# A hand-written planner learns to model three DMA queues, and takes its order of work from tables

## The chip, the cores and the metric

The kernel runs on one core of a Trainium2 chip. A core has five engines that run side by side, each through its own list of instructions in order: TensorE (PE: matmuls; its weight loads are shown as PEld), VectorE (DVE), ScalarE (ACT), GpSimd (POOL, which here only builds two index tiles and issues loads) and SyncE (SP, which here only issues stores and transposes by DMA). They wait for each other through semaphores. The metric is the device time of one execution in microseconds, lower is better.

## The reference

Causal attention with a sliding window and a few global keys, followed by a two-layer feed-forward net. Four batches, eight heads, 768 tokens, 64 numbers a head; 3072 tokens of width 512 go into the net, whose hidden width is 2048.

```python
scores = scale * np.matmul(q, k.transpose(0, 1, 3, 2))
keep = is_global | is_local              # 8 global keys, 96 keys back
scores = np.where(keep, scores + bias, -1000000000.0)
a = np.exp(scores - np.max(scores, axis=-1, keepdims=True))
a = a / (np.sum(a, axis=-1, keepdims=True) + 1e-09)
x = np.matmul(a, v)                      # to 3072 x 512
h = np.maximum(x @ w_in, 0.0)
out = h * h @ w_out
```

## The kernel before, in words

The 768 tokens of a batch are cut into six tiles of 128; three tiles make a half (eight halves, numbered 0 to 7, `hb` in the code). For a half, q and k are loaded (POOL, lines 395 on) and turned so that a head's 64 numbers lie on the partitions: halves 0, 1 and 2 on PE (`turn_tile`, `turn`), later ones by DMA transposes on SP's queue (`turn_by_dma`). `score_unit` multiplies q and k, ACT takes the exponential, DVE multiplies by a mask, `attend` multiplies with v, DVE divides by the sum (`norm`), and SP transposes the result by DMA into `xt` (`to_x_by_dma`, line 684). `layer1` multiplies by `w_in`, ACT or DVE take the positive part and the square; `layer2` multiplies by `w_out`, and SP stores. A part of layer 1 and most of layer 2 go through seven half-size products in place of eight (`layer1_group`, line 809, `layer2_pair`, line 1044), with sums of weights and of activations made by DVE.

The first two halves are done tile by tile (`OPENING`): `score_tile` first puts the distance bias into PSUM with matmuls of a diagonal (`slope_id`, line 1250) and then adds the scores (line 1257); `attend_tile`, `tile_to_x` (turned on PE) and pieces of layer 1 follow. `w_in` comes in four quarters (line 456).

Nobody writes the order of the instructions down: `Plan.run` does. It is a list scheduler that runs while the kernel is built. Every piece of work is an `Op` with a cost for each engine that could do it, what it needs, which ring of buffers and which of the eight PSUM banks it takes, and a rank. At each step the planner takes, among all ops whose needs are planned, the one that can start first by its own clock, with the rank as the tie-break, picks the engine that ends it first, and emits its instructions. PE's jobs and the loads are kept in two queues in the order in which they were listed (`merge`, `PLACES`, `LAYER1`, `OPENING`, `LOADING`), and only a queue's head can be planned. A DMA is modelled by a fixed lag, a fixed duration after the last one, and 2.8 us more when loads are under way (`crowd`). Before 24 us of the planner's clock, gaps in front of PE jobs are filled with dummy matmuls (`warm`, lines 281 and 284).

PE changes between matmuls that contract over 128 rows and the scores, which contract over 64 rows in pairs. Buffers named below: `ex`, `ph0` and `phat` hold weights of the attention, `hr` and `h2` the hidden layer, `y` the output, `w_mix` and `in_mix` sums of weights.

Of the kernel before, what the change touches and what calls it, by code (L numbers as in the profile page):

```python
# [13 lines left out]
P = 128  # L14
# [39 lines left out]

class Op:
    EARLY = {"ACT": 0.035, "DVE": 0.045}
    LATE = {"ACT": 0.1, "DVE": 0.07}

    def __init__(self, costs, emit, needs, rank=0, lag=0.0, land=None, slots=()):
        self.emit, self.rank, self.lag, self.land = emit, rank, lag, land  # L60
        self.needs = [n for n in needs if n is not None]
        self.costs = {e: c - self.EARLY.get(e, 0.0) for e, c in costs.items()}
        self.slots = slots
        self.done, self.bufs = None, []
        self.crowd = 0.0
        self.wait = 0.0
        self.shy = {}
# [12 lines left out]

class Plan:
# [8 lines left out]
    HOP = 0.08  # L90

    def __init__(self, warm_from, warm_until):
        self.warm_from, self.warm_until = warm_from, warm_until
        self.queues = {"PE": [], "LOAD": []}
        self.rest = []
        self.free = {e: 0.75 for e in ("ACT", "DVE", "POOL", "SP")}
        self.landed = 4.2
        self.rank = 0
        self.banks = [[] for _ in range(8)]
        self.rings = {}  # L100

    def pe(self, cost, emit, needs=(), takes=0, lag=0.24):
        self.rank += 1
        op = Op({"PE": cost}, emit, needs, self.rank, lag)
        op.takes, op.users = takes, [[op] for _ in range(takes)]
# [10 lines left out]
    def add(self, costs, emit, needs=(), rank=None, wait=0.0):  # L116
        rank = self.rank if rank is None else rank
        op = Op(costs, emit, needs, rank + RANKS.get(emit.__name__, 0))
        op.wait = wait
# [3 lines left out]
    def load(self, dur, emit, needs=(), rank=None, lag=2.6, hop=1.45):  # L123
        rank = self.rank + 0.5 if rank is None else rank
        op = Op({"POOL": 0.92}, emit, needs, rank, lag, land=dur)
        op.hop = hop
# [20 lines left out]
    def ready(self, op):  # L147
# [3 lines left out]
        for n in op.needs:  # L151
            if n.done is None:
                return None
            t = max(t, n.done + self.HOP)
        if getattr(op, "takes", 0):
# [11 lines left out]

    def run(self):
        order = []
        while self.rest or any(self.queues.values()):  # L170
# [13 lines left out]
            taken = self.idle_banks(op.takes) if getattr(op, "takes", 0) else []  # L184
            self.free[e] = end
            op.done = end + op.lag + op.LATE.get(e, 0.0)
            if op.crowd and self.landed > end + 0.3:
                op.done += op.crowd
                self.landed += getattr(op, "dma", 0.0)
            if op.land is not None:  # L190
                self.landed = max(end + op.hop, self.landed) + op.land
                op.done = self.landed + op.lag
# [20 lines left out]
def kernel(  # L213
# [169 lines left out]
    def list_loads(x, first=None):  # L383
# [5 lines left out]
        vbefore = [halves[x.hb - x.half - 3].attended[-1]] if x.hb >= 4 else []  # L389

        def rows(src, name, t, rank=None):
# [10 lines left out]
            if x.hb > 2:  # L402
                return plan.load(1.12, emit, vbefore if name == "v" else before, rank, 1.3, 0.7)
            return plan.load(0.86, emit, vbefore if name == "v" else before, rank,
                             1.6 if x.hb == 0 else 2.6)

        if x.half == 0:
# [3 lines left out]
            x.bt.op = plan.add({"DVE": 0.1}, start, vbefore, rank=0)  # L411
# [22 lines left out]
    def first_tiles(x, dst, src, eng, e, lags):  # L434
        casts = []
        for i, lag in enumerate(lags):
# [7 lines left out]
            op = plan.add({e: 0.5}, start, rank=-1)  # L444
            op.lag = lag
# [8 lines left out]
    def load_w_in(c):  # L454
        n = d_ff // 4
        w_in_op[c] = plan.load(2.55, lambda e: nc.gpsimd.dma_start(
# [3 lines left out]
    def list_w_out(first):  # L460
        n = NFT // 4
        for c in range(4):
            w_out_op.append(plan.load(2.55, lambda e, c=c: nc.gpsimd.dma_start(
# [33 lines left out]
    def fix_v(bt, t0, t1):  # L497
# [9 lines left out]
        if BY_DMA[2 * batches.index(bt) + t0 // HT]:  # L507
            op = plan.add({"SP": 1.2}, values_by_dma, needs, wait=4.0)
            op.lag, op.crowd, op.dma = 2.2, 2.8, 0.5
        else:  # L510
            op = plan.add({"DVE": 0.62} if bt is batches[0] else {"DVE": 0.62}, values,
                          needs, wait=0.0 if bt is batches[0] else 4.0)
# [36 lines left out]
    def turn_by_dma(x):  # L549
        late = list(halves[x.hb - 2].x_ops.values()) if x.hb > 3 else []  # L550
        for i, (name, loads) in enumerate((("sk", x.k_in), ("sq", x.q_in))):
# [7 lines left out]
            op = plan.add({"SP": 1.6}, emit, [*x.k_in, *x.q_in, x.bt.op, *late])  # L559
            op.lag = 3.4  # L560
# [3 lines left out]
        def fix(e):  # L564
# [5 lines left out]
                      x.turned[:1], wait=4.0)  # L570
# [12 lines left out]
    def score(x, k):  # L583
        for unit in [UNITS[x.half][u] for u in TOGETHER[x.half][k]]:
            score_unit(x, unit, unit[0] == UNITS[x.half][TOGETHER[x.half][k][0]][0])

    def score_unit(x, unit, fresh):
# [12 lines left out]
        job = plan.pe(0.182 * fresh + 0.057 * 4, emit,  # L600
                      [o for a in {a for a, _, _ in unit} for o in x.qk_ops[a]], 2)
# [76 lines left out]
    def to_x_by_dma(x, a):  # L678
# [8 lines left out]
        x.x_ops[a] = plan.add({"SP": 1.3}, emit, [norm])  # L687
        Buffer("tm", 6).used_by(norm, x.x_ops[a])
        x.xt_buf.used_by(x.x_ops[a])
        x.x_ops[a].lag, x.x_ops[a].crowd = 1.8, 2.8  # L690


    def layer1(x, ms, c0=0, c1=HALF, k0=0, k1=NCT):
# [3 lines left out]
        def emit(e):  # L697
            if x.h2 is None:
                x.h2 = h_p.tile([P, NFT, HALF], FP16, name="h2", tag="h2")
# [3 lines left out]
            for i, m in enumerate(ms):  # L703
                for kk in range(k0, k1):
# [6 lines left out]
                       for o in [x.x_ops.get((a, t), x.x_ops.get(a))]] + [w_in_op[ms[0] // 4]],  # L711
                      int(k0 == 0))
# [24 lines left out]
        if len(ms) > 1 or ms[0] % 2:  # L737
            m0 = ms[0] // 2 * 2 if len(ms) == 1 else ms[0]

            def square(e):  # L740
                hr = pair["hr"][:, 0:width * n].rearrange("p (m c) -> p m c", c=n)
                h2 = x.h2[:, m0:m0 + width, c0:c1]
# [52 lines left out]
    def layer1_group(x, g):  # L795
# [5 lines left out]
        def product(name, fresh, left, right, needs):  # L801
            def emit(e):
                if x.h2 is None:
                    x.h2 = h_p.tile([P, NFT, HALF], FP16, name="h2", tag="h2")
# [58 lines left out]
        def give(job, name, which, n, kept=None):  # L863
# [42 lines left out]
            def square(e):  # L906
                hr, h2 = hidden(which), x.h2[:, m0 + which * far:m0 + which * far + 2]
# [50 lines left out]
    def layer2(x, j, m0):  # L958
        st = x.l2.setdefault(j, {})

        def emit(e):
            if m0 == 0:
                st["ps"] = bank([P, 512], FP32, "yps")
            for m in range(m0, m0 + 4):
# [3 lines left out]
                      + [w_out_op[m0 // 4]], int(m0 == 0))  # L968
# [6 lines left out]
        if m0 + 4 == NFT:  # L975
# [5 lines left out]
            store = plan.add({"SP": 0.6}, lambda e: nc.sync.dma_start(  # L981
# [531 lines left out]
```

## Time and profile before

| what | us |
|---|---|
| median of 3 runs (203.25 to 204.84) | 203.93 |
| profiled execution, first to last instruction (span) | 202.3 |
| PE busy / DVE / ACT / POOL | 194.4 / 172.8 / 146.1 / 66.8 |
| first matmul starts (a dummy) | 1.67 |
| last matmuls (16 of line 1161) start | 198.08 |

The profiled execution is known by its span alone; the median of the runs lies 1.6 us above it. A PE matmul's own duration (273 ns for 128x256) is longer than its place in the stream, since matmuls are pipelined: eight of them that start at 196.33 are followed by the next eight at 197.21, so one takes 0.110 us of PE. Read the same way from rows that follow each other, a matmul takes 0.162 us of PE at 384 columns, 0.109 at 256, 0.082 at 192, 0.056 at 128, 0.216 at 512, 0.030 for the 65 columns of the attention, and 0.028 for one of the scores' pairs. The granted clock of PE was 1.00 over the traced span, but its first dummies follow each other at 0.106 us and, from 5.4 us on, at 0.056.

Busy shares by stretch, from the windows of the trace:

| us | PE | DVE | ACT | GB/s |
|---|---|---|---|---|
| 0 to 20 | 16.44 of 20 | 14.88 | 16.41 | 169 |
| 20 to 40 | 19.67 | 18.45 | 17.32 | 182 |
| 80 to 100 | 19.21 | 18.03 | 16.56 | 153 |
| 100 to 120 | 19.93 | 19.86 | 17.18 | 157 |
| 140 to 160 | 20.00 | 19.28 | 16.52 | 56 |
| 180 to 203 | 19.14 of 23 | 13.83 | 9.41 | 58 |

### The profile page before, as it was taken

How to read it: one execution, taken by the hardware profiler on the slowest of the kernel's cores; microseconds unless marked ns; L12 is line 12 of the kernel's file. 1: busy time of each engine (PE TensorE's matmuls, PEld its weight loads, DVE VectorE, ACT ScalarE, POOL GpSimd, SP SyncE). 2: the span in 40 equal slices, each digit the busy share in tenths (PEclk: the TensorE clock that was granted, in tenths of full speed). 3: DMA queues.
4: the chain of work that ended last, by engine and by line, in shares of the span. 5: the costliest groups of instructions: out<-in, count | busy, mean ns of one | idle time of the engine just before them, and what ended most of it. 6: DMA issues, size and time to landing. Idle time of an engine off the chain costs nothing.

```text
span 202.3 us, 5784 instructions
## 1 busy us (share of the span) xinstructions
PE 194.4 (96%) x2292; PEld 159.2 (79%) x2292; DVE 172.8 (85%) x455; ACT 146.1 (72%) x308; POOL 66.8 (33%) x82
## 2 busy tenths in 40 slices
PE   6798999999999999998999999999999999999993
PEld 6577887965897777777788878997788788987883
DVE  7569979999996798987999999998899979288922
ACT  6799998699522999968888797748886952478220
POOL 7996638077009600940680059000000000000000
PEclk9999999999999999999999999999999999999999
DMA  5999999999999998999999999993232023110123
GB/s 161 176 150 191 198 178 155 199 206 163 176 162 143 204 182 168 108 181 170 156 134 157 162 169 134 161 173 84 41 105 75 3 66 99 52 55 0 52 107 104
DMA packets 106491, 27.12 MB, mean 134 GB/s; under 512 B 96992, under 2 KB 103520, under 8 KB 106464
## 3 DMA queue, kind: packets, MB, share of 16 engines
q0 software_dynamic: 74944, 13.11, 91.2%
q1 hardware_dynamic: 30320, 13.05, 32.0%
q10 hardware_dynamic: 1200, 0.59, 1.1%
q8 instruction: 18, 0.29, 0.6%
q14 instruction: 9, 0.07, 0.1%
HBM read 27.26 MB, written 6.29 MB: 166 GB/s over the span
## 4 chain that ended last, share of the span: by engine, by line
PE 74%; DMA 12%; DVE 6%; POOL 4%; issue 1%; ACT 0%; POOLq 0%; DVEq 0%
PE yps L1044 31%; PE hps L705 21%; PE hps L809 11%; DMA w_in_sb<-in_moe_w_in_dram 6%; PE sp L598 4%; DMA w_mix<-in_q_dram 4%; PE av L659 3%; PE yps L965 3%; DMA xt<-tm 2%; POOL v L395 1%; POOL w_mix L395 1%; DVE hr L867 1%; DVE h L746 1%; PE trp L535 1%; DVE tm L669 1%
## 5 line engine op out<-in xcount | busy, mean ns | idle before, releaser
L705 PE MATMUL hps<-xt,w_in_sb 128*128 128x384 f16 (+2 forms) x432 | 62.8, 290 | 1.0 <-DVE tm L669 0.7
L705 PEld LDWEIGHTS <-w_in_sb 128*128 128x128 f16 x432 | 36.8, 98 | 13.8 <-DVE tm L669 0.9
L730 ACT ACTIVATE hr<-hps 128x384 f16<-128x384 f32 (+1 forms) x73 | 37.1, 519 | 9.1 <-PE hps L705 8.3
L264 ACT COPY y<-yps 128x256 f32<-128x256 f32 (+2 forms) x41 | 15.7, 384 | 30.2 <-PE yps L1044 25.6
L611 ACT ACTIVATE ex<-sp 128x512 f16<-128x512 f32 x66 | 34.7, 621 | 2.7 <-PE sp L598 2.6
L1044 PEld LDWEIGHTS <-h 128*128 128x128 f16 x344 | 32.9, 98 | 4.7
L395 POOL DMA_DIRECT2D sk<-in_k_dram x19 | 16.8, 895 | 50.9 <-DMA q<-sq 44.4
L1044 PEld LDWEIGHTS <-mixed 128*128 128x128 f16 x264 | 25.3, 98 | 3.4
L395 POOL DMA_DIRECT2D v<-in_v_dram x24 | 21.6, 919 | 3.6 <-DMA w_in_sb<-in_moe_w_in_dram 1.6
L1099 DVE TENSOR_TENSOR y<-yps,y 128x256 f32<-128x256 f32 x31 | 13.0, 418 | 10.8 <-PE yps L1044 7.1
L1044 PE MATMUL yps<-w_out_sb,h 128*128 128x256 f16 x176 | 21.9, 273 | 0.0
L1044 PE MATMUL yps<-w_mix,h 128*128 128x256 f16 x168 | 21.8, 273 | 0.0
L1044 PE MATMUL yps<-w_mix,mixed 128*128 128x256 f16 x176 | 21.7, 273 | 0.0
L635 DVE TENSOR_TENSOR phat<-ex,mask 128x1024 f16<-128x1024 f16 (+1 forms) x36 | 20.7, 593 | 0.0
L867 DVE TENSOR_TENSOR hr<-hps,kept 128x384 f16<-128x384 f32 x32 | 16.9, 548 | 2.6 <-PE hps L809 2.3
L395 POOL DMA_DIRECT2D sq<-in_q_dram x19 | 17.0, 916 | 3.0 <-DVE vb L266 1.7
L264 ACT COPY kept<-hps 128x384 f32<-128x384 f32 x30 | 13.6, 485 | 6.0 <-PE hps L809 6.0
L744 ACT ACTIVATE h<-hr 128x768 f16<-128x768 f16 (+1 forms) x21 | 16.4, 782 | 0.3
L809 PEld LDWEIGHTS <-in_mix 128*128 128x128 f16 x176 | 14.9, 98 | 1.9
L809 PE MATMUL hps<-x_mix,in_mix 128*128 128x192 f16 x132 | 14.8, 246 | 0.0
L669 DVE TENSOR_TENSOR tm<-av,rec 128x384 f16<-128x384 f32 x24 | 13.4, 557 | 0.9
L746 DVE TENSOR_TENSOR h<-hr 128x768 f16<-128x768 f16 (+1 forms) x27 | 13.1, 498 | 0.8 <-ACT hr L730 0.8
(110 smaller groups left out, 336.3 us busy)
## 6 DMA issues: line engine op xcount, KB each, us to landing
out_dram<-y SPq DMA_DIRECT2D x23, 256.0 KB, 2.4
v<-in_v_dram POOLq DMA_DIRECT2D x24, 128.0 KB, 7.6
sq<-in_q_dram POOLq DMA_DIRECT2D x19, 128.0 KB, 6.8
sk<-in_k_dram POOLq DMA_DIRECT2D x19, 128.0 KB, 5.8
w_in_sb<-in_moe_w_in_dram POOLq DMA_DIRECT2D x4, 512.0 KB, 10.8
w_out_sb<-in_moe_w_out_dram POOLq DMA_DIRECT2D x4, 512.0 KB, 10.1
y<-in_k_dram ACTq DMA_DIRECT2D x2, 256.0 KB, 4.9
y<-in_q_dram SPq DMA_DIRECT2D x2, 256.0 KB, 4.3
```

The lines of the kernel that those rows point to most:

```text
L264: nc.scalar.copy(out=out, in_=in_)
L395: dma = nc.gpsimd.dma_start(out=dst, in_=src[x.b, :, r0 + t * P:r0 + (t + 1) * P, :] .rearrange("h p d -> p h d"))
L611: nc.scalar.activation(out=st["ex"][:, h], in_=sp[h], func=AF.Exp, scale=scale)
L635: eng(e).tensor_tensor(out=x.phat[a][:, :, t0:t0 + n], op=ALU.mult, in0=st["ex"][:, :, i0:i0 + 2 * n].rearrange("p e (t b) c -> p e t (b c ...
L669: nc.vector.tensor_tensor(out=st["tm"].rearrange("p t e d -> p e t d"), in0=av[:, :, :, 0:D], in1=rec[:, :, :, None].to_broadcast([P, 2, H ...
L705: nc.tensor.matmul(st["ps"][:, i * n:(i + 1) * n], lhsT=w_in_sb[:, kk, m * P:(m + 1) * P], rhs=x.xt[:, kk, c0:c1], start=kk == 0, stop=kk ...
L730: nc.scalar.activation(out=o, in_=i, func=AF.Relu)
L744: nc.scalar.activation(out=h2, in_=hr, func=AF.Square)
L746: eng(e).tensor_tensor(out=h2, in0=hr, in1=hr, op=ALU.mult)
L809: nc.tensor.matmul(st[name][:, i * HC:(i + 1) * HC], lhsT=left(i, kk), rhs=right(kk), start=fresh and i == kk == 0, stop=kk == KK - 1, ski ...
L867: eng(e).tensor_tensor(out=hidden(which)[:, :, cols], in0=sums(name), in1=st[kept], op=ALU.add)
L1044: nc.tensor.matmul(st[bank_name][:, 0:HN], lhsT=a(m), rhs=b(m), start=fresh and m == 0, stop=m == HK - 1, skip_group_check=not fresh)
```

## The change

All of it is in the planner and in what it is told; the set of useful matmuls, loads, transposes and stores stays the same.

1. Three tables, `PE_ORDER`, `LOAD_ORDER` and `REST_ORDER`, hold the numbers of the ops. `arrange` sorts PE's queue and the load queue by them, and gives every other op its place in the third table as its rank.
2. `Transfers` models the queues of POOL, SP and ACT: a transfer starts a while after its issue, shares the DMA engines with the heads of the other queues by weights, and is done a while after. It replaces `lag`, `land`, `crowd` and `landed`.
3. PE jobs carry a mode (128 rows or 64), and a change of mode costs 0.095 or 0.12 us; the flat 0.182 us of a first score unit is gone. Other costs are set anew.
4. `score_tile` is cut in two PE jobs: the matmuls of the diagonal (`slope`), which need no q or k, and the scores.
5. `squares_of` makes the `h2` tile at the first square and not at the first matmul of layer 1; `ph0` is made at its first write. `vbefore` waits for two more halves' worth of `attend` jobs. PE jobs that share a bank name the one before them as a need.

```diff
+PE_ORDER = """73 49 64 50 60 61 56 74 65 68 86 87 84 79 77 69 92 97 101 90 114 107 105 99 116 109 135 123 130
...
+LOAD_ORDER = """14 13 16 18 17 15 21 12 20 23 19 22 24 25 27 26 29 28 228 230 231 229 232 233 235 237 234 239
...
+REST_ORDER = """362 1076 353 1044 894 702 54 323 203 305 526 120 622 210 521 982 160 522 429 776 162 415 95 253
...
+class Transfers:
+    KINDS = {"load": (0.91, 0.95, 1.56, 1.64), "weights": (1.01, 2.4, 0.57, 1.8),
+             "store": (0.55, 0.85, 0.8, 0.6), "turn": (0.46, 1.68, 0.02, 0.75),
+             "turn_x": (0.31, 1.1, 0.7, 0.5), "first": (1.07, 0.7, 1.36, 0.87)}
...
+    def issue(self, engine, start, end, op):
+        self.step(self.queues, self.now, start)
+        self.now = start
+        before, work = self.KINDS[op.dma][:2]
+        self.queues[engine].append([end + before, work, op.dma, op])
...
+    SWITCH = {(P, P): 0.0, (P, P // 2): 0.095, (P // 2, P // 2): 0.0, (P // 2, P): 0.12}
...
+    def arrange(self):
+        ops = {op.number: op for op in [*self.queues["PE"], *self.queues["LOAD"], *self.rest]}
+        for key, table in (("PE", PE_ORDER), ("LOAD", LOAD_ORDER)):
+            self.queues[key] = [ops.pop(int(i)) for i in table.split()]
+        for op in self.queues["PE"]:
+            op.rank = -1
+        self.rest = [ops.pop(int(i)) for i in REST_ORDER.split()]
+        for i, op in enumerate(self.rest):
+            op.rank = i
...
     def run(self):
+        self.arrange()
...
-            op.done = end + op.lag + op.LATE.get(e, 0.0)
-            if op.crowd and self.landed > end + 0.3:
-                op.done += op.crowd
...
+            if op.dma:
+                self.transfers.issue(e, start, end, op)
+            else:
+                op.done = end + op.lag + op.LATE.get(e, 0.0)
...
-        job = plan.pe(0.182 + NPAIR * 0.07 + added * H * 0.056, emit, needs, 2)
+        first = added and plan.pe(H * 0.056, slope, slope_ops, 2)
+        if added:
+            slope_buf.used_by(first)
+        job = plan.pe(NPAIR * 0.057, emit, needs + [first] * added, 0 if added else 2, mode=(D, D))
```

In the built program the loads of q, k and v for halves 0 and 1 come in this order (k2 is k of tile 2, c1 is the second quarter of `w_in`). Before: v1 q2 k2 k3 q3 v0 v2 q5 q4 k4 k5 c1 v3 c0 v4 c3 c2 v5. After: k2 q2 q3 v2 v0 k3 k4 v1 q4 c1 q5 k5 v3 c0 c3 v4 v5 c2. PE has 2251 matmuls after and 2292 before: the useful ones are the same 2236, the dummies go from 56 (54 of 128 columns) to 15 (9 of 512 columns, 6 of 128). PE changes between 128 and 64 rows 42 times after and 46 times before. The last matmuls before are the 16 of line 1161, which write the last quarter of the last tile's output; after, these 16 come 24 matmuls ahead of the end, and the last eight write half of another tile's output row, whose 256 KB store is then the last.

More of the change, by code (lines that the diff above doesn't have):

```diff
@@ L153, in ready @@
                 return None
-            t = max(t, n.done + self.HOP)
-        if getattr(op, "takes", 0):
+            if "PE" not in n.costs or "PE" not in op.costs:
+                t = max(t, n.done + self.HOP)
+        if op.takes:
             banks = self.idle_banks(op.takes)
@@ L183, in run @@
             idle = self.free.get(e, self.warm_from)
-            taken = self.idle_banks(op.takes) if getattr(op, "takes", 0) else []
+            taken = self.idle_banks(op.takes) if op.takes else []
+            if e == "PE":
+                end += self.SWITCH[self.mode, op.mode[0]]
+                self.mode = op.mode[1]
             self.free[e] = end
-            op.done = end + op.lag + op.LATE.get(e, 0.0)
-            if op.crowd and self.landed > end + 0.3:
-                op.done += op.crowd
[L189 to L192, printed above, removed]
+            if op.dma:
+                self.transfers.issue(e, start, end, op)
+            else:
+                op.done = end + op.lag + op.LATE.get(e, 0.0)
             for q in self.queues.values():
@@ L401, in emit @@
                     x.last_load = dma
[L402 to L405, printed above, removed]
+            return plan.load("load", emit, vbefore if name == "v" else before, rank)
         if x.half == 0:
@@ L1246, in emit, with slope @@
             warm(pair[0].rearrange("p a c -> p (a c)"))
[L1247 to L1251 removed]
+            return pair
+        def slope(e):
+            pair = banks()
+            for a in range(NPAIR):
+                for h in range(2):
+                    nc.tensor.matmul(pair[h][:, a, :], lhsT=slope_id[:, 2 * a + h, :],
+                                     rhs=dmask16[:, c0:c0 + P], start=a == 0, stop=False)
+        def emit(e):
+            pair = st["sp", before] if added else banks()
             for a in range(NPAIR):
```

182 lines of the change are left out of this document (111 added, 71 removed), and 44 rows, old and new, of tables (PE_ORDER, REST_ORDER).

## The prediction

> **What bounds the kernel now.** I read the page's busy shares, then the stream of matmuls (PE's timeline), PE's waits, the loads on POOL and the transposes on SP.
>
> ```profile
> span 202.3 us, 5784 instructions
> PE 194.4 (96%) x2292; PEld 159.2 (79%) x2292; DVE 172.8 (85%) x455; ACT 146.1 (72%) x308; POOL 66.8 (33%) x82
> PE 74%; DMA 12%; DVE 6%; POOL 4%; issue 1%; ACT 0%; POOLq 0%; DVEq 0%
> ```
>
> PE is the bound. Its useful work, by places in the stream: 384 columns 240 x 0.162, 256 columns (96+608) x 0.109, 192 columns 308 x 0.082, 128 columns 248 x 0.056, 512 columns 32 x 0.216, attention 352 x 0.030, scores 352 x 0.028: 182.5 us. The change leaves all of it, so only the other 19.8 us of the span can move. PE's timeline shows the start:
>
> ```profile
> 1.67 4.23 PE L284 MATMUL trp<-ident,early 128*128 128x128 f16 x41 [1.67 <-DVE ident L308]
> ...
> 6.59 0.40 PE L1205 MATMUL trp<-ident,sq 128*128 128x128 f16 x4 [0.24 <-DVE sq L266]
> 7.49 0.40 PE L1205 MATMUL trp<-ident,sk 128*128 128x128 f16 x4 [0.51 <-ACT sk L264]
> 7.73 0.89 PE L284 MATMUL trp<-ident,early 128*128 128x128 f16 x13
> 8.70 0.40 PE L1205 MATMUL trp<-ident,sq 128*128 128x128 f16 x4
> 9.61 0.40 PE L1205 MATMUL trp<-ident,sk 128*128 128x128 f16 x4 [0.51 <-DMA sk<-in_k_dram]
> 9.85 0.61 PE L1250 MATMUL sp<-early,slope_id 128*128 128x128 f16 x8
> 10.39 0.40 PE L1257 MATMUL sp<-q,k 64*128 64x128 f16 x8
> ```
>
> Until 9.6 us PE has done 20 transposes and waits for loads; tile 2's turn, the last of these rows, stands ahead of the first scores at 10.39. A change of mode is in the last two rows: the last diagonal starts at 9.85 + 7 x 0.056 = 10.24, the first score 0.15 later in place of 0.056, so a change costs 0.095.
>
> The second look is at the loads, on POOL's timeline and in the summary of the tile `w_in_sb`:
>
> ```profile
> 1.67 1.04 POOL L395 DMA_DIRECT2D v<-in_v_dram  x1 [0.40 <-DVE ident L308]
> 11.44 0.83 POOL L456 DMA_DIRECT2D w_in_sb<-in_moe_w_in_dram  x1
> 16.43 0.74 POOL L456 DMA_DIRECT2D w_in_sb<-in_moe_w_in_dram  x1 [0.83 <-DMA w_mix<-in_q_dram]
> ```
> ```profile
> DMA to landing us min/median/max: 8.3/10.8/12.6
> ```
>
> The first quarter of `w_in` lands at 11.44 + 8.3 = 19.7, and layer 1 starts at 19.80; the last one lands at 16.43 + 12.6 = 29.0. The loads land one after another: v1 at 7.90, and ten tiles later, at 17.34, k5: 0.94 a tile; the quarters then 3.4 apart with a tile between two: 2.4 each.
>
> Third, the x transposes on SP and the end of the stream:
>
> ```profile
> L684 SPq DMA_TRANSPOSE xt<-tm x24: 1179/1204/1981, 57.5 to 167.5; - x24
> DMA to landing us min/median/max: 2.3/3.6/6.9
> ```
> ```profile
> out_dram<-y SPq DMA_DIRECT2D x23, 256.0 KB, 2.4
> out_dram<-y SPq DMA_DIRECT2D x1, 64.0 KB, 1.6
> ```
> ```profile
> 198.08 1.06 PE L1161 MATMUL yps<-w_mix,h 128*128 128x128 f16 x16
> 198.35 0.42 DVE L1099 TENSOR_TENSOR y<-yps,y 128x256 f32<-128x256 f32 x1 [0.46 <-PE yps L1044]
> 198.80 0.33 SPq L1109 DMA_DIRECT2D out_dram<-y  x1
> ```
>
> **The account of the 19.8 us.** Before the first turn of half 2 (line 535, 39.91 us) PE has 27.2 us of useful work behind it: 12.7 lost, of which 22 changes of mode are 2.1. From there to the end of the matmuls at 198.98, 155.3 are useful and 3.8 lost: 24 changes (2.3) and holes, of which three are seen, 0.28 at 87.3, 0.84 at 95.0 and 0.24 at 100.1: 1.4. After the last matmul 3.3. Together 19.8.
>
> **Part 1, the opening.** The new order was walked by hand, with landings at 0.94 a tile and 2.4 a quarter. The first load no longer waits 0.40 for DVE's memset of v, so k2 lands at 7.5 to 7.9, and with nine tiles ahead of it (9 x 0.94 of landings less one) c1 lands at 17.4 to 17.8 (before 19.7), k5 at 19.3 (before 17.3), c0 22.6, c3 25.0, v5 26.9 and c2 at 29.3 to 29.7 (before 29.0).
>
> The diagonals go first: 8 of the 40 stand before any turn and 16 more between the first turns, where PE waits for loads now. The first scores need tile 0 and 1 alone: the last cast at 6.80 (the landing that ACT's cast waited for now) + 0.85 for two casts on DVE, 0.45 of turns, 0.5 + 0.5 for two copies on ACT, so about 9.6 in place of 10.39. ACT's 22 exponentials (0.51 apart) begin that much earlier. From c1 at 17.6, PE has ahead of the c2 jobs: layer 1 pieces 0.89 x 3 + 0.87 x 6, the turn 0.45, attention 1.45, scores 0.45, x turns 0.78 and two changes: 11.2, and a wait for k5 of 0.7 (the turn of tile 5 stands one piece after c1's first). That makes 29.5, just when c2 lands. On DVE the masks of tile 5 (its exponentials end near 25.4, four masks of 0.41 and two squares of 0.4 behind them) and the copy of v4 end near 27.9, 0.5 after PE would want them, so I take 30.0. Then 5.7 of layer 1 to the first turn of half 2: 35.7, and 36.0 with 0.3 for PSUM banks that ACT frees late (it is busy 0.9 of this stretch). Useful work behind PE there is 25.0, so 11.0 are lost in place of 12.7: **-1.7**. Bounds: c2 at 29.3 without the other waits, -2.5; 1 us more of ACT's lag, -0.7. The 14 changes of mode (1.3) are inside. The 41 dummies that go cost nothing and save nothing: PE waits in their place.
>
> **Part 2, changes of mode in the rest.** 28 in place of 24: 4 x 0.095 = **+0.4**.
>
> **Part 3, holes in the rest.** 1.4 now. The planner now charges late transposes, so holes could close; but it also packs tighter. In PE work from the last `attend` of a half to its first layer 1 job on all columns: half 2 8.3 (before 10.8), half 3 9.0 (10.7), half 4 7.0 (10.8), half 6 8.5 (11.4), half 7 9.8 (13.0). The path across costs 0.36 for the attention, 0.74 on DVE (0.19 + 0.56), 1.2 behind another transpose on SP, 3.6 to land: 5.9, so it fits everywhere at the median; at 6.9 it is 9.2 and does not fit in four. Bounds 0 and 5.8 of holes (the slower rival); I take 1.0, near the row of now since the median fits: **-0.4**.
>
> **Part 4, the end.** Now the last piece is 64 KB: from the last start, 198.98 - 0.06, copy at 199.50, issue at 199.79, landing 1.6 later. After: the last eight of 256 columns are followed, like those that start at 197.21, by a DVE addition 0.38 after the last start, an SP issue 0.45 later (198.35 to 198.80) and 2.0 to 2.4 for 256 KB: 2.8 to 3.2 in place of 2.5. **+0.4**, bounds +0.3 and +1.0 (it may meet the store issued 2.2 earlier).
>
> **Part 5, the rest of the edits.** The new order of SP puts a half's x transposes behind the next half's two turns (k, q), as now. `squares_of` and the wider `vbefore` only move when a buffer is taken; the loads of q and k wait for turns, and those of v have their half's whole stage. Cost 0; the cover is POOL's idling between halves (44.4 us in 4 waits for `q<-sq`); without it each microsecond that a half's loads lose comes off the slack before its scores.
>
> Sum: 202.3 - 1.7 + 0.4 - 0.4 + 0.4 = 201.0 of span. The median of the runs lies 1.6 above the profiled span: **202.6**, 0.7% faster. A measurement of this kernel can tell about 1% from no change.
>
> [...] The first dummies follow each other at 0.106 us, and at 0.056 from 5.4 us on, 3.7 after PE's start; holes of 0.5 to 0.7 after that did not bring 0.106 back. After the change PE's holes before c1 are longer (about 1.5 us around the second turns of tile 0, some 3.5 in all until 17.6). A relapse to 0.106 for as long as the start took, 3.7 us, would make 1.85 us of work late: 202.6 + 1.85 = 204.4, the rival "relapse". [...]
>
> **Rivals.**
> - *The loads are the only limit, and holes close* (-2.5 + 0.4 - 1.4 + 0.3 = -3.2): 200.7. For it: c1 lands 2 us earlier, three holes are all that the rest has now. Against: ACT and DVE are at 0.9 in 20 to 40 us.
> - *Given back*: the opening gains 1.7, but the packed middle waits for DVE (19.86 of 20 us busy at 100 to 120), and holes grow by 1.7 over now, in place of -0.4: 202.3 - 1.7 + 0.4 + 1.7 + 0.4 = 203.1 of span, 204.7. Against: DVE's work is the same within 1 us.
> - *Slower: x transposes land late.* Place: the start of layer 1 in halves 2, 4, 6 (and 3). Against 7.0 to 9.0 us of PE work, a landing at 6.9 makes the path 9.2: holes of 0.9, 2.2, 0.7 and 0.2, and at half 2, whose first mixed product stands only 6.5 after the `attend` that it needs, 2.7 in place of 0.9: 5.8 in all, 4.8 above my 1.0: 207.4. It decides from landings of 4.7 at half 4 (7.0 - 2.3) and 5.9 on average; the price passes 1% at about 3.4 of extra holes. For it: the longest now are 6.9, those issued while POOL's loads run. Against: the median is 3.6.
>
> **Chances and numbers.** Forecast 0.42, loads alone 0.28, given back 0.14, slower 0.13, relapse 0.03. Within 1% is 201.9 to 206.0. Faster takes loads alone and a small part of the forecast: 0.32; slower takes 0.13 and a bit of the two middle rivals: 0.15; the same: 0.53. The range reaches past loads alone (200.7) to 200.5 and into the slower case as far as half of its holes, 205.6. The forecast's own range is 201.8 to 203.6.
>
> **What would show it.** Right: the first score near 9.6 and the first layer 1 matmul at 17.5 to 18.3; the first turn of half 2 at 35.5 to 36.7; 42 changes of mode; holes after that of about 1 in all; 2.8 to 3.2 from the last matmul's start to the last landing. Wrong: c1 landing after 18.5, PE holes at 60 to 65 or 100 to 104 us that end with `xt<-tm`, or matmuls 0.106 apart after 8 us.

## The result, and the profile after

The changed kernel takes 204.36 us (median of 22 runs, 203.51 to 206.9) and the kernel before 203.31 (22 runs, 202.67 to 204.84) on the same chip: ratio 1.0050, 95% interval 1.0033 to 1.0068. One of the 22 executions after, the one of 206.9, was in a slower state and is not in the ratio. The changed kernel is slower by half a per cent, and the whole interval lies above 1; the forecast was 202.6 and 0.7% faster. In the four executions of these two kernels where a time stands beside a profile, the time is 1.76 to 1.77 above the span, so the medians are spans of about 201.5 before and 202.6 after: the execution shown of before (202.3) took 0.8 longer than the median, and its account has to be read with two further profiles of the same kernel (203.3 and 201.7) and one more of the changed one (203.3).

The page of the changed kernel, span, busy shares and the chain:

```profile
span 202.5 us, 5683 instructions
PE 194.3 (96%) x2251; PEld 157.2 (78%) x2251; DVE 174.7 (86%) x455; ACT 145.3 (72%) x308; POOL 67.0 (33%) x82
PE 74%; DVE 11%; DMA 6%; ACT 5%; issue 1%; ACTq 0%; DVEq 0%
```

PE's share of the chain is 74% as before; DVE's grew from 6 to 11 and DMA's fell from 12 to 6: PE now waits less for loads and more for DVE. The raw tiles of q and k, as loaded, are `sq` and `sk`; `trp` and `trx` are PSUM tiles of turns. The opening, PE's timeline (start, duration, instruction, count, idle time and what ended it):

```profile
8.14 0.61 PE L1366 MATMUL sp<-early,slope_id 128*128 128x128 f16 x8
9.71 0.40 PE L1376 MATMUL sp<-q,k 64*128 64x128 f16 x8 [0.96 <-DVE k L381]
...
14.47 0.40 PE L1376 MATMUL sp<-q,k 64*128 64x128 f16 x8 [0.46 <-ACT k L379]
...
17.41 1.14 PE L1376 MATMUL sp<-q,kb 64*128 64x128 f16 x16 [0.31 <-ACT q L379]
...
19.23 0.27 PE L1460 MATMUL trx<-ident,tm 128*128 128x128 f16 x2 [0.18 <-ACT ex L1402]
19.34 1.06 PE L818 MATMUL hps<-xt,w_in_sb 128*128 128x128 f16 x16
```

The first score is at 9.71 (10.39 before). On POOL the first load goes out at 1.37 (1.67 before), and c1, issued at 9.83, lands 7.8 later, at 17.6 (19.7 before):

```profile
1.37 1.04 POOL L511 DMA_DIRECT2D sk<-in_k_dram  x1
...
9.83 0.78 POOL L568 DMA_DIRECT2D w_in_sb<-in_moe_w_in_dram  x1
```

But layer 1 starts at 19.34 only (19.80 before). PE's order is fixed, and ahead of layer 1 stand three scores (the first two in the row at 17.41) and two turns, of which some wait for ACT. ACT copies `xt` only from 17.74 on, behind the copy of a turn, for which it had waited for DVE, and an exponential:

```profile
16.77 0.59 ACT L379 COPY q<-trp 128x512 f16<-128x512 f16 x1 [0.39 <-DVE k L381]
17.25 0.60 ACT L1402 ACTIVATE ex<-sp 128x512 f16<-128x512 f32 x1
17.74 0.93 ACT L379 COPY xt<-trx 128x256 f16<-128x256 f16 x3
18.52 2.13 ACT L1402 ACTIVATE ex<-sp 128x512 f16<-128x512 f32 x4
```

In the middle the largest hole is at 110.57, in the attention of half 5. On PE it looks so:

```profile
110.57 0.19 PE L770 MATMUL av<-v,phat 128*128 128x65 f16 x1
111.42 0.19 PE L770 MATMUL av<-vb,phat 128*128 128x65 f16 x1 [0.66 <-DVE vb L381]
```

Its cause starts on POOL. The first of these loads waits 14.1 for the turn of `sq`; the three loads of v that half 5 needs (the two at 101.29 and the one at 103.89) are queued behind it, and the last lands at 110.42:

```profile
100.43 0.88 POOL L511 DMA_DIRECT2D sq<-in_q_dram  x1 [14.11 <-DMA q<-sq]
101.29 1.77 POOL L511 DMA_DIRECT2D v<-in_v_dram  x2
...
103.89 0.92 POOL L511 DMA_DIRECT2D v<-in_v_dram  x1
...
108.21 0.96 POOL L511 DMA_DIRECT2D sk<-in_k_dram  x1
109.08 1.85 POOL L511 DMA_DIRECT2D v<-in_v_dram  x2
```

DVE then has to copy v into `vb` while POOL issues the rest of that burst. Elsewhere such a copy takes 0.28; here the first two take 1.61 (0.74 and 0.83):

```profile
107.28 1.36 DVE L746 TENSOR_TENSOR phat<-ex,mask 128x1024 f16<-128x1024 f16 x3
108.55 1.61 DVE L381 COPY vb<-v 128x520 f16<-128x520 f16 x2
110.09 0.33 DVE L901 TENSOR_TENSOR x_mix<-xt,x_mix 128x384 f16<-128x384 f16 x1
110.35 0.41 DVE L1130 TENSOR_TENSOR mixed<-h,mixed 128x512 f16<-128x512 f16 x1
110.68 0.68 DVE L381 COPY vb<-v 128x520 f16<-128x520 f16 x2
```

The x transposes are no later than before (2.3/3.6/6.9 there):

```profile
DMA to landing us min/median/max: 2.3/3.4/7.0
```

And the end, last matmuls, last addition, and the row of the page for the stores:

```profile
198.07 1.04 PE L1157 MATMUL yps<-w_out_sb,h 128*128 128x256 f16 x8
199.14 0.42 DVE L1212 TENSOR_TENSOR y<-yps,y 128x256 f32<-128x256 f32 x1 [0.45 <-PE yps L1157]
```
```profile
out_dram<-y SPq DMA_DIRECT2D x23, 256.0 KB, 3.1
```

From the last matmul's start (198.83) to the end of the span it takes 3.69; before, 3.38 (from 198.92 to 202.29). The last store lands 2.77 after that start; before, 2.48.

**The account.** I cut each profile at the point where 20 us of useful matmuls are behind PE (about where half 2 begins to matter), and count as holes what PE loses after it beyond useful work (at 182.5 for the whole, as in the prediction) and changes of mode (0.096 each):

| us | before (shown) | before, 2nd | before, 3rd | after (shown) | after, 2nd |
|---|---|---|---|---|---|
| span | 202.3 | 203.3 | 201.7 | 202.5 | 203.3 |
| 20 us of useful work done at | 32.56 | 33.06 | 33.15 | 31.92 | 32.01 |
| changes of mode after that | 2.3 | 2.3 | 2.3 | 2.7 | 2.7 |
| holes after that | 1.68 | 2.15 | 0.44 | 1.94 | 2.60 |
| last matmul's start to the end | 3.38 | 3.41 | 3.42 | 3.69 | 3.69 |

### The profile page after: what moved, and what is told of

It is laid out like the page before. It is cut to its first block, busy times and chain, and to the rows that moved or that the text cites. A ratio compares the mean times of both kernels' runs of the same rounds, so it can differ in the third digit from the quotient of the medians.

```text
span 202.5 us, 5683 instructions
## 1 busy us (share of the span) xinstructions
PE 194.3 (96%) x2251; PEld 157.2 (78%) x2251; DVE 174.7 (86%) x455; ACT 145.3 (72%) x308; POOL 67.0 (33%) x82
## 4 chain that ended last, share of the span: by engine, by line
PE 74%; DVE 11%; DMA 6%; ACT 5%; issue 1%; ACTq 0%; DVEq 0%
PE yps L1157 28%; PE hps L818 22%; PE hps L921 9%; PE av L770 4%; DMA xt<-tm 3%; PE yps L1078 3%; PE sp L709 3%; DMA y<-in_k_dram 3%; DVE vb L381 2%; DVE phat L746 2%; ACT ex L722 1%; ACT ex L1402 1%; DVE hr L979 1%; DVE x_mix L901 1%; PE sp L1376 1%
## 5 line engine op out<-in xcount | busy, mean ns | idle before, releaser
L844 ACT ACTIVATE hr<-hps 128x384 f16<-128x384 f32 (+1 forms) x75 | 38.9, 539 | 19.4 <-PE hps L818 18.9
L818 PEld LDWEIGHTS <-w_in_sb 128*128 128x128 f16 x432 | 37.5, 98 | 12.9 <-issue 0.2
L722 ACT ACTIVATE ex<-sp 128x512 f16<-128x512 f32 x66 | 35.6, 628 | 3.9 <-PE sp L709 3.8
L379 ACT COPY y<-yps 128x256 f32<-128x256 f32 (+2 forms) x43 | 16.3, 379 | 19.2 <-PE yps L1157 16.7
L511 POOL DMA_DIRECT2D sk<-in_k_dram x19 | 17.3, 916 | 18.0 <-DMA k<-sk 12.5
L1157 PE MATMUL yps<-w_mix,mixed 128*128 128x256 f16 x176 | 22.4, 273 | 0.0
L1157 PE MATMUL yps<-w_mix,h 128*128 128x256 f16 x168 | 21.3, 273 | 0.0
L860 DVE TENSOR_TENSOR h<-hr 128x768 f16<-128x768 f16 (+1 forms) x36 | 17.7, 502 | 2.6 <-ACT hr L844 2.2
L921 PE MATMUL hps<-x_mix,in_mix 128*128 128x192 f16 x132 | 15.6, 246 | 0.1
L921 PEld LDWEIGHTS <-w_in_sb 128*128 128x128 f16 x132 | 11.4, 98 | 1.4
```

Source lines behind the costliest of these rows:

```text
L379: nc.scalar.copy(out=out, in_=in_)
L511: dma = nc.gpsimd.dma_start(out=dst, in_=src[x.b, :, r0 + t * P:r0 + (t + 1) * P, :] .rearrange("h p d -> p h d"))
L722: nc.scalar.activation(out=st["ex"][:, h], in_=sp[h], func=AF.Exp, scale=scale)
L818: nc.tensor.matmul(st["ps"][:, i * n:(i + 1) * n], lhsT=w_in_sb[:, kk, m * P:(m + 1) * P], rhs=x.xt[:, kk, c0:c1], start=kk == 0, stop=kk ...
L844: nc.scalar.activation(out=o, in_=i, func=AF.Relu)
L860: eng(e).tensor_tensor(out=h2, in0=hr, in1=hr, op=ALU.mult)
```

## The experiments

The theory when I began: the tables put the v loads of half 5 behind a waiting q load, which makes the hole at 110; the opening is held by ACT and no longer by loads. The rival: DVE is full in the packed middle, and whatever is moved, its work ends late.

**1. The v loads first.** In `LOAD_ORDER`:

```diff
-... 425 427 540 426 535 539 538 536 537 682 543 541 680 542 683 ...
+... 425 427 426 540 535 539 538 536 537 543 541 542 682 680 683 ...
```

> In the load table, the last v tile of half 4 and the three of half 5 are put ahead of the next half's first q load, which waits 12 to 14 us for a turn. Nothing else is edited. If the table's place for these loads makes the hole of 0.82 us at 110.6 us (the attention of half 5 waits for the copy of v, whose load landed at 110.4), the hole goes, the span falls by 0.5 to 1.0 us and the ratio to before is 0.998 to 1.002. Rival: DVE, 9.85 of 10 us busy there, is late by itself; then a hole of 0.5 us or more stays in 105 to 115 us and the ratio stays at 1.003 to 1.007.

Measured: ratio 1.0097 (1.0062 to 1.0131). The hole at 110 is gone, and a new one of 1.0 stands at 99, where the copies went. PE and DVE there:

```profile
100.39 0.82 PE L919 MATMUL hps<-x_mix,w_in_sb 128*128 128x192 f16 x8 [0.84 <-DVE hr L977]
```
```profile
97.88 0.61 DVE L379 COPY vb<-v 128x520 f16<-128x520 f16 x2
...
99.27 0.61 DVE L379 COPY vb<-v 128x520 f16<-128x520 f16 x2
99.80 0.54 DVE L977 TENSOR_TENSOR hr<-hps,kept 128x384 f16<-128x384 f32 x1
```

The copies now take their 0.3 each, but stand on DVE ahead of the `hr` that PE needs. The late loads make the hole at 110; they are not what the time hangs on. The rival's cause (DVE) fits so far; its place (105 to 115) and its ratio (1.003 to 1.007) do not.

**2. Half the exponentials in the opening.** Only the first half of the columns of each exponential of halves 0 and 1 is computed, and what follows reads that half twice.

```diff
-                nc.scalar.activation(out=o[:, h], in_=st["sp", before][h], func=AF.Exp, scale=scale)
+                nc.scalar.activation(out=o[:, h, 0:2], in_=st["sp", before][h][:, 0:2], func=AF.Exp, scale=scale)
```

> The changed kernel with the exponentials of halves 0 and 1 over half of the columns (the other half of the heads' weights is left out and the written half is read in its place); order and everything else as in the changed kernel. If ACT bounds the opening, layer 1 starts at c1's landing, 17.6 to 18.4 us in place of 19.34, and the first turn of half 2 stands at 35.2 to 36.0 in place of 36.84. If the loads bound it, both stay within 0.3 us.

Measured: one time, 204.07. Layer 1 started at 19.11 and the first turn of half 2 came at 36.69, against 19.34 and 36.84; 20 us of useful work were done at 31.77 (31.92). That is less than 0.3 each, as expected if the loads bound it. But in this execution PE waited for a cast that took 0.79 in place of 0.41:

```profile
8.24 0.40 PE L1318 MATMUL trp<-ident,sq 128*128 128x128 f16 x4 [0.83 <-DVE sq L381]
```

The same wait stands in the profiles of runs 1, 3, 13 and 14, which have the same opening with whole exponentials: there layer 1 starts at 19.50 to 19.72, and 20 us of useful work are done at 32.20 to 32.59, 32.42 on average. Against these, half the exponentials gain about 0.65, on a single profile. So the exponentials hold a part of the opening. They are not alone: layer 1 still started after the 17.6 to 18.4 expected, and PE's wait of 0.46 for ACT's copy of k (at 14.47 above) is there too. The opening is a chain of small waits through ACT, DVE and the first landings in an order that is fixed.

**3. The old end.** The 64 KB store is the last again:

```diff
-... 1138 1125 1070 1140 1142 1157 1144 1164 1162 1168 1147 1177 1174 1159 1171 1166"""
+... 1138 1125 1070 1140 1142 1157 1144 1164 1162 1168 1147 1159 1171 1166 1177 1174"""
```

> In PE's table the two jobs of the last quarter tile (16 matmuls) go back behind the other 24, so that the last stores are 64 KB again. If the tail is mis-sized in the planner, the stretch from the last matmul's start to the end of the span falls from 3.7 to 3.4 us and the ratio by 0.001 to 0.002 against the changed kernel (1.005), to about 1.003. Rival: the stores share the engines and the tail stays at 3.6 to 3.8.

Measured: ratio 1.0046 (1.0018 to 1.0074). The end takes 3.41 (3.69), as expected, and a hole of 0.68 appears ahead of it:

```profile
195.93 1.03 PE L1157 MATMUL yps<-w_mix,h 128*128 128x256 f16 x8 [0.51 <-DVE y L1212]
```

So the price of the end was right (0.28), but in the tables' order the pieces that stand there give DVE time for `y`: nothing is won by moving them back.

**4 to 6. Tables and model apart.** No tables (the call of `arrange` is removed); tables for the opening alone, the rest in the listed order with the old ranks; and the reverse.

```diff
-        self.arrange()
```
```diff
-            self.queues[key] = [ops.pop(int(i)) for i in table.split()]
+            table = table.split()
+            first = [ops[int(i)] for i in table[:table.index(cut)]]
+            self.queues[key] = first + [op for op in self.queues[key] if op not in first]
...
+        for i, n in enumerate(REST_ORDER.split()):
+            if int(n) < 227:
+                ops[int(n)].rank = i - 2000
```

The third has `last` from the cut on in place of `first`, and the ranks from 227 on.

> The call that sorts by the tables is taken out; the new model of transfers, costs and the split of the first scores stay, and the order is the listed one with the old ranks. If the model alone plans better, 0.995 to 1.000 of before. Rival: the old ranks fit the old model, and the stretch after the first turn of half 2 loses more in holes than before's 1.7 to 2.2 us; then 1.003 to 1.015.

> The changed kernel's planner, with the tables for the opening alone (PE's jobs up to the first turn of half 2, the first 18 loads, the ranks of the other ops of that part); everything behind it in the order in which it is listed, with the ranks of before. Theory: the opening by tables gains about 0.5 us, and the middle by tables gives it back in changes of mode, holes and the tail; then this lies at 0.994 to 0.999 of before. Rival: the new cost model, or the opening, is what costs time; then 1.003 or more.

> The reverse: the opening in the listed order with the old ranks, everything from the first turn of half 2 on by the tables. Theory (the middle costs): 1.005 to 1.012 of before, with 28 changes of mode after the first turn and a tail of 3.7 us. Rival (the opening costs): 1.002 or less.

Measured: 1.0243 (1.0190 to 1.0296), 1.0287 (1.0223 to 1.0351) and 1.0366 (1.0328 to 1.0403). Runs 4 and 6 lie above both ranges that were expected; run 5 falls to its rival (1.003 or more). The new model with the old order costs 2.4%, and the tables win most of it back. The rest's tables alone are worse than none; for the opening's the intervals overlap. PE loses 6.6, 6.0 and 8.1 after the opening (1.94 and 2.60 in the changed kernel), and the largest parts are single holes: 1.99 at 106 (and 1.77 at 59) without tables, 4.16 at 81 (scores that wait for a turn on SP) with the opening's, 2.62 at 114 with the rest's. The largest hole of each run is followed by slow matmuls, which the last section takes up; in 5:

```profile
85.11 0.50 PE L708 MATMUL sp<-q,k 64*128 64x128 f16 x6 [4.09 <-DMA q<-sq]
...
86.50 2.75 PE L1156 MATMUL yps<-w_out_sb,h 128*128 128x256 f16 x16
```

Cut at this place, the order can't be divided into a good and a bad part. The opening without tables (runs 4 and 6) has 20 us of useful work done at 32.57 and 32.44, with all 22 changes of mode.

**7 to 9. Less work for DVE, in both kernels.** The big copies of v into `vb` are left out in halves 2 to 7, and the attention reads v itself (so the global keys are missing there). First one execution of the changed kernel (7), then both kernels timed (8 the changed one, 9 the one before).

```diff
-            copy(e, bt.vb[:, t0 - 1:t1 - 1], bt.v[:, t0:t1])
+            if bt is batches[0]:
+                copy(e, bt.vb[:, t0 - 1:t1 - 1], bt.v[:, t0:t1])
...
-                    rhs = (bt.vb[:, r - 2, 2 * a + h, :] if before and r > 1
-                           else bt.v[:, r - before, 2 * a + h, :])
+                    rhs = bt.v[:, r - before, 2 * a + h, :]
```

> The changed kernel, same order, without the large copy of v to vb in halves 2 to 7 (the attention of these reads v in its place, so their global keys are left out): 14 copies of about 0.36 us less on DVE. If DVE's queue, and not a single transfer, makes the holes after the first turn (1.9 us in the changed kernel), they fall below 1.0 us. Rival: they wait for transposes and loads; then 1.5 or more stay.

> The changed kernel again without the big copies of v in halves 2 to 7 (the attention reads v itself there, so the global keys are left out), now timed. The one look gave a span of 201.7 and 203.49 us, 0.8 less than the changed kernel's profile. Theory (the packed middle of the new order has no slack on DVE, and that is what its median loses against before): 203.4 to 203.7, ratio to before 1.000 to 1.002, and the kernel before gains nothing like it from the same relief. Rival (DVE is as full in both orders and both gain the same): the same 203.4 to 203.7 here, but before with the same relief lies at 202.3 to 202.7, so that the difference between the two stays near 1.0.

> The kernel before with the same leaving-out as in the changed one (no big copies of v in halves 2 to 7, global keys left out there). The planner is free to reorder here, since no table holds the order. Theory (only the new order suffers from DVE): ratio to before 0.998 to 1.002, its hole of 0.8 at 95 us stays. Rival (both orders suffer alike): ratio 0.995 to 0.997, that hole is gone.

Measured: the one execution took 203.49, with 1.1 of holes after the opening, between the two values expected; 12 copies are gone (DVE has 443 instructions in place of 455), not 14. Timed: the changed kernel 203.06, ratio to before 0.9974 (0.9953 to 0.9995); the kernel before with the same relief 203.09, 0.9977 (0.9962 to 0.9992). So the copies cost the changed kernel about 0.8% (1.0050 to 0.9974) and the kernel before 0.2%, and without them the two are equal. Both expectations were half right: before gains too, but a third as much. The changed kernel's opening is as in its own profile (31.93), and its holes after it are 0.5 in place of 1.9 and 2.6. The page of the timed one:

```profile
span 201.1 us, 5672 instructions
PE 193.5 (96%) x2251; PEld 157.0 (78%) x2251; DVE 170.4 (85%) x443; ACT 145.5 (72%) x308; POOL 67.1 (33%) x82
```

This places the loss: it lies on those copies, in the order that the tables give. The other terms of the account confirm it: opening, changes of mode and end come to -0.1 together (see below), and without the copies the two kernels differ by 0.03. Leaving a copy out takes away DVE's time for it and also PE's wait for its result; these runs do not tell the two apart.

**10 to 12. Both kernels again, for more profiles.**

> The kernel before, unchanged, for a second profile. If the holes of 0.84 and 0.28 us at 95 and 87 us are accidents of the profiled execution, they are gone and the span is 201.2 to 201.8; if they belong to the order, they are there again and the span is 202.0 to 202.5.

> The kernel before once more, for a third profile. Its two profiles so far have spans of 202.3 and 203.3, while its median corresponds to about 201.5 (the median less the 1.78 between time and span). If these two were merely late executions, a third is expected at 201.3 to 202.3, with the time saved in the opening (20 us of useful work done by 31.5 to 32.5, in place of 32.56 and 33.06) and in the holes at 87 to 101.

> The changed kernel once more, for a second profile. If the end of its first layer 1 wait (first layer 1 matmul at 19.3) and its hole of 0.8 at 110 us belong to the order, both come again within 0.3 us of where they were, and the opening at 20 us of useful work lies at 31.9 to 32.4; if they were a matter of that one execution, they move.

Measured: before 205.05 and 203.44, after 205.04, with the accounts in the table above. The second profile of before fits neither expectation: its span is 203.3, and holes of 0.73, 0.64 and 0.45 end at 88.6, 96.6 and 101.3. In the second of the changed kernel layer 1 starts at 19.42, and the hole in the attention of half 5 is there again (1.07, at 111). The third profile of before is short because its middle has almost no holes, and not, as I had expected, also because of its opening. In its opening a hole of 1.29 stands where the execution shown had 0.51:

```profile
16.92 0.40 PE L1257 MATMUL sp<-q,k 64*128 64x128 f16 x8 [1.23 <-DVE k L266]
```
```profile
13.64 1.46 DVE L266 COPY vb<-v 128x520 f16<-128x520 f16 x2 [0.17 <-DMA v<-in_v_dram]
```

Again two copies of v that take 1.46 in place of 0.6.

**13 and 14. The copies of half 5 on ACT**, in `fix_v`; then the same with the loads of 1.

```diff
+            late = bt is batches[2] and t0 >= HT - 1
-            op = plan.add({"DVE": 0.62} if bt is batches[0] else {"DVE": 0.62}, values,
+            op = plan.add({"ACT": 0.95} if late else {"DVE": 0.62}, values,
```

> The copies of v of half 5 (three tiles, two copies each) are put on ACT, the loads stay late, nothing is left out. DVE theory: the waiting attention of half 5 goes earlier by what stands ahead of the copies on DVE, the hole at 110 us shrinks from 0.8 to 1.1 to under 0.4, ratio to before about 1.000 to 1.003. Loads theory: the last v lands at 110.4 whatever engine copies it, so the hole stays at 0.6 or more and the ratio at 1.004 to 1.008. ACT theory (ACT is busy 9.2 of 10 us at 100 to 110 and has its own things to do for PE): a new hole of 0.5 or more behind ACT's kept or hr, ratio above 1.005.

> The copies on ACT as in e10 and the loads of v ahead of the waiting loads of q as in e1, so that they come at about 97 to 100 us, where ACT is busy 7.4 of 10. Both needed: no hole above 0.4 between 95 and 115, span 201.4 to 202.0, ratio to before 0.997 to 1.001, the fastest of the versions that compute everything. ACT theory or something else behind it: ratio 1.004 or more, with a hole of 0.5 or more behind ACT between 95 and 105.

Measured: 1.0240 (1.0208 to 1.0272) and 1.0086 (1.0055 to 1.0116). On ACT a copy took 0.62; the hole at 110 shrinks to 0.46 in the first and is gone in the second, and in its place come 1.05 at 87 and 2.17 at 129 (waiting for `y` on DVE) in the first, and 1.03 at 88 (the third x transpose of half 4, issued at 82.90 while POOL issues loads, lands at 89.23) in the second. No new hole of 0.3 or more ends with ACT, so a full ACT is not shown. Ahead of the hole at 129 the chain of work that ended last runs through DVE alone, from 123.73 to 131.37 with less than 0.7 unaccounted: DVE is full there although the copies of half 5 had left it. The hole behind an x transpose at 87 to 89 is not of this edit alone: it also stands in runs 2, 7, 9 and 10 (0.48 to 1.04), and so in both kernels.

**15 and 16. Another form of the copy.** DVE makes the copies as a maximum of the source with itself, by `tensor_tensor`: the four of half 5, then all into `vb` and those into `kb` of halves 0 to 2.

```diff
+        elif twice:
+            nc.vector.tensor_tensor(out=out, in0=in_, in1=in_, op=ALU.max)
```

> The four copies of half 5 (two tiles) are made by DVE as a tensor_tensor maximum of v with itself, which gives the same values. Theory (a copy waits for the load that POOL is issuing, a tensor_tensor does not): each of the four takes 0.41 to 0.44 whatever POOL does, in place of 0.74, 0.83, 0.36 and 0.28 (0.44, 0.83, 0.30 and 0.84 in the second profile). The sum falls from 2.2 to 2.4 to 1.7, but the last v lands at 110.4 only, so the hole at 110 keeps 0.6 to 0.9: ratio to before 1.002 to 1.006. Rival (whatever reads v there is slowed, by the landing of loads or by POOL): they take 0.6 or more in this form too.

> All copies into vb, those into kb in halves 0, 1 and 2, in the same other form: 0.42 in place of 0.28 at 520 columns, about 0.35 in place of 0.24 at 384. What is lengthened on DVE falls from 6.5 to about 3.9, but 32 copies of v and about 14 of k get 0.1 to 0.14 longer, so DVE's work grows by about 2. Theory that the waits count where they fall (opening and half 5): ratio to before 0.998 to 1.004, 20 us of useful work done by 31.3 to 31.9. Theory that DVE's sum counts: ratio 1.006 to 1.012, with new holes behind DVE between 60 and 130.

Measured: 1.0049 (1.0026 to 1.0073) and 1.0066 (1.0038 to 1.0094). DVE in the first, at the place shown above:

```profile
108.71 0.88 DVE L381 TENSOR_TENSOR vb<-v 128x520 f16<-128x520 f16 x2
...
110.30 0.88 DVE L381 TENSOR_TENSOR vb<-v 128x520 f16<-128x520 f16 x2
```

Each takes 0.42, and the hole at 110 is 0.48, less than the 0.6 to 0.9 expected. In the second all 32 take 0.42 to 0.43, sixteen of them while POOL issues a load. So of the two forms of the copy only the plain one was lengthened beside POOL's loads. The time does not move: 0.42 everywhere costs as much as 0.28 with some at 0.8, and what this hole gives up is lost elsewhere. No version that computes everything beats the kernel before.

## Why the prediction was wrong, point by point

**Part 1, the opening (-1.7).** The loads came as worked out (first score 9.71 for 9.6, c1 at 17.6), but layer 1 did not start with c1: 19.34, above the 17.5 to 18.3 given, and the first turn of half 2 at 36.84, above 35.5 to 36.7. The step that failed is the sentence "From c1 at 17.6, PE has ahead of the c2 jobs": it takes PE as ready at c1, with 0.3 for ACT. PE's order is fixed, and ahead of layer 1 it has three scores and two turns that wait for ACT, which itself waits for DVE. A misreading adds to it: near 39.91 stands the first turn of k in half 2, but the first turn of all, of q, starts at 39.75. So 12.5 were lost there and not 12.7, and the gain, by the prediction's own working, would have been 1.5. Over nine profiles that share the new opening, 20 us of useful work are done at 32.2 on average (31.92 to 32.59); over the three of the kernel before and the one of run 9, at 33.0 (32.56 to 33.26): a gain of 0.8. By the sum, the eight changes of mode that the opening is spared make 0.77 of that: the waits moved from loads to ACT and DVE and stayed as long. But runs 4 and 6 come to 32.57 and 32.44 without the tables' opening and with none of these changes spared, so not all of the 0.8 is owed to the tables.

**Part 2, changes of mode (+0.4).** Right: 28 in place of 24 after the opening, +0.38.

**Part 3, holes in the rest (1.0 in place of 1.4).** Wrong in sign: 1.94 and 2.60 against 1.68, 2.15 and 0.44, so 2.3 against 1.4 on average, +0.85. The step that failed is the choice of the path: I argued from the x transposes alone, which land as before; the largest hole is in the attention of half 5, behind the copies of v, and without these copies 0.5 of holes are left (run 8; 1.1 in run 7). That is also where **Part 5 (zero)** fails: "those of v have their half's whole stage" is false in a queue in order. The loads of v stand behind a load of q that waits 14.1, and the last of them lands 0.2 before PE stops. The cover that I named, POOL's idling, is that very wait. What this alone costs is not shown: with the loads moved up (run 1) the hole at 110 went, and the time did not fall.

**Part 4, the end (+0.4, bounds +0.3 and +1.0).** +0.29: at the lower bound.

**The sum.** -0.80 + 0.38 + 0.85 + 0.29 = +0.72, where -1.3 was forecast; of these 2.0, Part 3 makes 1.25 and Part 1 0.9. Between the medians lie +1.05 (0.67 to 1.38 by the interval). The difference of 0.33 stays open: two and three profiles do not average the holes well. The useful work, with the factors as they are printed, adds up to 182.1 and not 182.5; every hole count would be 0.4 larger with it, in both kernels alike. The level was off too: by adding 1.6 from a median of three runs to the one profiled execution, I set the time before 0.6 too high.

**The rivals.** What came is "given back", to which I gave 0.14 and 204.7: an opening that gains, a packed middle that waits for DVE, and holes that eat more than the gain. Runs 7 to 9 bear out its mechanism (as far as the copies of v go), its terms were too large on both sides. The slower rival's transposes did not land later. "Relapse" did not happen in the changed kernel, whose holes after 8 us stay at 1.1 and below; it did in runs 4 to 6 and 13, by holes of 2 us and more.

## What to carry to other kernels

Ask of each load which load stands ahead of it in its queue and what that one waits for: the loads of v, without a need of their own, stood here behind a wait of 14.1. In an order that is packed until PE, DVE and ACT are nine tenths busy, as here from 100 to 110, a relief at one place came back as loss at another in all five attempts at the middle that compute everything (runs 1 and 13 to 16). Take a second and third profile of the kernel before before setting up a sum of terms under 1 us: here two executions of the same program differ by 1.6 in span, and one wait in the opening by 0.8.

## What the runs showed of the hardware

**Copies on DVE that began in the middle of a load's issue on POOL were lengthened to its end.** The copies of v (520 columns on 128 or, for the global keys, on 32 partitions, f16) in the changed kernel: 18 that meet no load instruction of POOL take 0.28, at most 0.30; 14 that meet one take 0.45 on average and up to 0.83. In all eighteen profiles, the 88 that took more than 0.33 end 0.08 to 0.12 after the end of a load instruction on POOL, like the second of those at 108.55, which ends at 110.16, 0.11 after the load issued at 109.08. Whether a copy is lengthened goes with its start. Of the 208 copies that meet a load, the 84 that start before it or up to 0.22 after its start take at most 0.30; the 63 that start 0.30 to 0.65 after its start are all lengthened. In the changed kernel's profile both stand side by side. The first copy below starts 0.15 after the load and takes 0.29; the second starts 0.47 after it, takes 0.53 and ends at 61.75, 0.09 after the first load's end:

```profile
60.75 1.79 POOL L511 DMA_DIRECT2D sq<-in_q_dram  x2 [10.62 <-DMA q<-sq]
60.90 0.85 DVE L381 COPY vb<-v 128x520 f16<-128x520 f16 x2
```

The casts of the first tile were lengthened too: in run 3 the cast of `sq` takes 0.89, where the changed kernel's profile has 0.41:

```profile
5.05 0.43 DVE L381 CAST sk<-y 128x512 f16<-128x512 f32 x1 [0.37 <-DMA y<-in_k_dram]
5.39 0.89 DVE L381 CAST sq<-y 128x512 f16<-128x512 f32 x1
```

These waits fall differently in each execution. Of the changed kernel's opening, the profiles with such a long cast (runs 1, 3, 13 and 14) have 20 us of useful work done at 32.2 to 32.6, those without (the two of the changed kernel, runs 5, 7 and 8) at 31.9 to 32.0; run 15, without one, has 32.45 behind another wait for a copy. A `tensor_tensor` of the same size was not lengthened (0.42 to 0.43, 32 of 32 in run 16). Why the two forms differ is not shown.

**After the four holes of 1.99 us and more the granted clock fell to half.** After the hole of 2.17 in run 13, PE's granted clock (the third number from the right; the first column is the stretch) falls, 3.1 after the hole began, and stays at half for 3.4 us:

```profile
129.00:132.00 3.00, 0.99 (x10) 0.73 (x9) 2.63 (x6) 0.37 (x1) 2.39 (x3) 1.00 2.38 156
132.00:135.00 3.00, 3.00 (x29) 1.94 (x27) 0.18 (x1) 2.26 (x5) 0.00 (x0) 0.56 2.14 203
135.00:138.00 3.00, 3.00 (x41) 2.54 (x40) 2.87 (x8) 1.40 (x4) 0.00 (x0) 0.87 0.61 115
```

The holes of 1.99, 4.16 and 2.62 in runs 4 to 6 were followed by it too (0.60 over 109 to 113, 0.50 over 85 to 87 and 0.50 over 116.6 to 119.6), one of 1.77 in run 4 was not. In the 3.4 us at half clock PE lost 1.5 to 1.7 more each time, so a hole of 2 us was paid almost twice, and part of what runs 4 to 6 and 13 lost is this.
